# Two kinds of early work moved to VectorE, with a new order of steps, in a fused DeltaNet and feed-forward kernel

## The chip, the cores and the metric

The kernel runs on one core of one Trainium2 chip. The metric is device time in microseconds (us), the median of several executions. Every execution used below for a ratio is in the fast state. A ratio is the mean time of one kernel's fast runs over the mean of the other kernel's fast runs of the same rounds on the same chip, with a 95% interval; it is therefore not quite the ratio of the medians that stand beside it. The kernel before had medians of 611.4 to 614.0 us in the different rounds, so ratios, not medians, are compared across experiments.

## The reference

```python
# q, k, v: (4, 8, 768, 48); beta: (4, 8, 768)
k_n = k / (np.linalg.norm(k, axis=-1, keepdims=True) + 1e-06)
for t in range(S):
    y[:, :, t] = np.einsum('bhd,bhde->bhe', q[:, :, t], state)
    v_old = np.einsum('bhde,bhd->bhe', state, kt)
    state = state + bt[:, :, :, None] * np.einsum('bhd,bhe->bhde', kt, vt - v_old)
# x = y as (3072, 384)
h = (x @ w1) * (x @ w2) @ w3        # w1, w2: 384 x 1024; w3: 1024 x 1024
out = h @ w_out                     # w_out: 1024 x 384
```

The kernel computes the recurrence in 12 chunks of 64 steps. Each chunk needs the inverse of a triangular matrix, built from the scores of K with K (called U). It folds w3 and w_out into one matrix w3·w_out before the feed-forward products start.

## The kernel before

The kernel is a set of named generators. Each `yield` ends a step, and a long string ORDER says in which order the steps are emitted. Every engine then executes its own instructions in that order, as the traces show: in the changed kernel ScalarE ran a copy of w3T at 39.70 us, the three passes of P10 at 40.90 to 42.02 and the second copy of Vb at 42.57, as ORDER has them. The names that matter here: K, Q (transposes), s (scores), V (the inverse of a pair of chunks, "V0" for the first), P0 to P7 (pieces of w_out), P8 to P23 (pieces of w3), t (transpose of a w3 piece), f (fold), p (loads of K and Q in a permuted layout, `kperm` and `qperm`), a (the first feed-forward products, `ab`).

A piece of a weight passes through four engines:

```python
def piece(n, srcs, dst):
    raw = in_turn(ffn, [P, CW, 2], "raw", 5, "raw", U32)
    for rows, src in srcs:
        sync.dma_start(...)                                      # SP's queue
    yield
    ...
    act.activation(out=dst, in_=hi..., func=ACTF.Abs, ...)       # ScalarE, three passes
    act.activation(out=lo, in_=lo, func=ACTF.Copy, ...)
    act.activation(out=hi..., in_=hi..., func=ACTF.Sign)
    yield
    dve.tensor_scalar(out=du, in0=du, scalar1=3, ..., op0=ALU.logical_shift_left)   # VectorE
    yield
    pool.tensor_tensor(out=du, in0=du, in1=lo, op=ALU.add)       # POOL
    pool.tensor_tensor(out=dst, in0=dst, in1=hi..., op=ALU.mult)
    yield
```

The inverse of the first pair runs on VectorE in PSUM, after two ScalarE copies that bring its start matrix Vb there. They are **two separate steps** of the order:

```python
def inverse(j):
    pool.memset(Vb[:], 0.0); ...                                 # step 1
    yield
    sync.dma_start(out=U[:], in_=Uds.pop(j)[:])                  # step 2: Ub
    yield
    if j < 2:
        V = two_banks()...
        for i in range(0, BS, BS // 2):
            act.copy(out=V[:, i : i + BS // 2], in_=Vb[...])     # steps 3 and 4
            yield
    for s in range(BS - 1):                                      # 31 steps of two VectorE operations
        dve.tensor_tensor(out=tv, in0=V[...], in1=U[...], op=ALU.mult)
        dve.tensor_tensor(out=o, in0=o, in1=tv, op=ALU.subtract)
        yield
    ...
```

In ORDER of the kernel before, the two copies are neighbours: `V0 V0`.

## Time and profile before

| | before |
|---|---|
| median (4 runs) | 611.37 us (610.85 to 614.12) |
| span of the profiled run, clock | 608.8 us, 0.969 |
| PE busy, idle | 569.2 us, 39.6 us |
| VectorE, ScalarE, POOL busy | 323.8, 183.4, 145.0 us |
| first inverse step on VectorE | 41.85 us |
| first `ab` product | 130.69 us |

Three readings carry the rest. PE's busy time is the work, as long as it took at the clock that was granted. Span minus PE busy is idle time (the prediction's 39.8 counts to 609.0 us), and all but 4.8 us of it lies in the first 180 us. In a timeline line, the first two numbers are start and duration of a group of equal instructions; the brackets at its end hold the idle time of that engine just before, and what ended it. The prediction below shows the profile's lines themselves; two that it lacks are the first inverse step and the first fold product (VectorE, then PE, of the kernel before):

```profile
41.85 0.19 DVE L434 TENSOR_TENSOR tb<-ps_w,Ub 128x31 f32<-128x31 f32 x1 [1.22 <-DMA Ub<-Ud]
...
45.74 4.77 PE L722 MATMUL ps_f<-w2s,w3T 128*128 128x384 f32 x8 [0.47 <-ACT w3T L716]
```

One warning on the clock columns, here and in the prediction: the trace's records of the granted clock begin only at 22.3 us in the kernel before and at 26.7 us in the changed kernel, and the views print 1.00 where there is no record. TensorE was slow there all the same: in the changed kernel a w3 transpose took 418 ns at 10 us, 417 ns at 39 us, where the record says 0.50, and 273 ns at 28 us, where it says 1.00.

### The profile page before, as it was taken

How to read it: one execution, taken by the hardware profiler on the slowest of the kernel's cores; microseconds unless marked ns; L12 is line 12 of the kernel's file. 1: busy time of each engine (PE TensorE's matmuls, PEld its weight loads, DVE VectorE, ACT ScalarE, POOL GpSimd, SP SyncE). 2: the span in 40 equal slices, each digit the busy share in tenths (PEclk: the TensorE clock that was granted, in tenths of full speed). 3: DMA queues.
4: the chain of work that ended last, by engine and by line, in shares of the span. 5: the costliest groups of instructions: out<-in, count | busy, mean ns of one | idle time of the engine just before them, and what ended most of it. 6: DMA issues, size and time to landing. Idle time of an engine off the chain costs nothing.

```text
span 608.8 us, 17988 instructions
## 1 busy us (share of the span) xinstructions
PE 569.2 (94%) x7804; PEld 333.2 (55%) x7804; DVE 323.8 (53%) x752; ACT 183.4 (30%) x373; POOL 145.0 (24%) x150
## 2 busy tenths in 40 slices
PE   3728998989999999999999999999999999999997
PEld 3724666644566545566555655566545564654454
DVE  2659975578745954766964539675384231101100
ACT  3677656754451012211102321123210113121100
POOL 5778866576340010200031001310000000000000
PEclk9856997999999999999999999999999999999999
DMA  9678678868764342725444354253102110000001
GB/s 200 163 192 230 189 144 172 200 143 156 135 124 86 88 81 27 124 51 111 95 88 64 48 109 99 54 84 60 48 21 86 31 33 1 27 29 13 1 13 39
DMA packets 202223, 55.67 MB, mean 91 GB/s; under 512 B 192352, under 2 KB 195424, under 8 KB 202144
## 3 DMA queue, kind: packets, MB, share of 16 engines
q1 hardware_dynamic: 197952, 53.74, 41.7%
q10 hardware_dynamic: 4192, 0.79, 1.0%
q8 instruction: 61, 1.00, 0.7%
q14 instruction: 18, 0.15, 0.1%
HBM read 42.30 MB, written 11.01 MB: 88 GB/s over the span
## 4 chain that ended last, share of the span: by engine, by line
PE 71%; DMA 8%; SPq 8%; DVE 6%; POOL 2%; issue 2%; ACT 1%; POOLq 0%; DVEq 0%; ACTq 0%
PE ps_f L742 36%; PE ps_f L762 21%; SPq L226 4%; PE ps_w L517 4%; PE ps_w L618 3%; DMA raw<-in_moe_w_dram 2%; PE ps_t L487 2%; SPq L663 2%; PE ps_w L366 2%; PE ps_t L473 1%; PE ps_w L360 1%; DVE ps_w L439 1%; DVE tb L434 1%; DMA Ub<-Ud 1%; DVE w L675 1%
## 5 line engine op out<-in xcount | busy, mean ns | idle before, releaser
L742 PE MATMUL ps_f<-xT,w2s 128*128 128x512 f32 x288 | 132.7, 600 | 0.2 <-POOL w2s L678 0.2
L742 PE MATMUL ps_f<-xT,w1s 128*128 128x512 f32 x288 | 131.1, 598 | 1.6 <-DMA xT<-xT 1.6
L762 PE MATMUL ps_f<-w,ab 128*128 128x384 f32 x384 | 127.3, 488 | 0.0
L762 PEld LDWEIGHTS ps_f<-w,ab 128*128 128x128 f32 x384 | 72.3, 190 | 50.9 <-issue 3.8
L756 DVE TENSOR_TENSOR ab<-a,ps_f 128x512 f32<-128x512 f32 x48 | 32.8, 686 | 126.0 <-PE ps_f L742 123.6
L742 PEld LDWEIGHTS ps_f<-xT,w1s 128*128 128x128 f32 x288 | 53.4, 190 | 62.9 <-issue 56.6
L742 PEld LDWEIGHTS ps_f<-xT,w2s 128*128 128x128 f32 x288 | 52.8, 190 | 59.3 <-issue 55.5
L751 ACT COPY a<-ps_f 128x512 f32<-128x512 f32 x48 | 27.5, 585 | 144.8 <-PE ps_f L742 140.5
L266 POOL TENSOR_TENSOR sq<-ktok 128x384 f32<-128x384 f32 x24 | 20.6, 858 | 156.5 <-DVE ss L268 98.9
L722 PE MATMUL ps_f<-w2s,w3T 128*128 128x384 f32 x128 | 48.9, 536 | 2.1 <-ACT w3T L716 2.1
L503 POOL TENSOR_TENSOR vtok<-vtok,n 128x384 f32<-128x384 f32 x24 | 19.6, 836 | 128.7 <-DMA vtok<-in_v_dram 128.7
L434 DVE TENSOR_TENSOR tb<-Vb,Ub 128x31 f32<-128x31 f32 (+15 forms) x124 | 43.5, 351 | 7.1 <-DMA Ub<-Ud 3.1
L639 ACT COPY xT<-ps_w 48x256 f32<-48x256 f32 x96 | 30.4, 365 | 50.1 <-PE ps_w L618 35.3
L439 DVE TENSOR_TENSOR Vb<-Vb,tb 128x31 f32<-128x31 f32 (+15 forms) x124 | 43.0, 347 | 4.3
L768 ACT COPY osb<-ps_f 128x384 f32<-128x384 f32 x24 | 11.4, 479 | 109.6 <-PE ps_f L762 81.5
L722 PEld LDWEIGHTS ps_f<-w2s,w3T 128*128 128x128 f32 x128 | 25.8, 209 | 19.9 <-issue 3.9
L360 PE MATMUL ps_w<-KQ 48*64 48x128 f32 x384 | 30.9, 306 | 3.9 <-ACT KQ L343 3.4
L360 PEld LDWEIGHTS ps_w<-KQ 48*64 48x64 f32 x384 | 25.8, 152 | 9.7 <-ACT KQ L343 4.0
L366 PE MATMUL ps_w<-KQ 48*64 48x64 f32 x768 | 30.9, 241 | 0.0
L581 DVE TENSOR_TENSOR S<-S,ps_w 48x768 f32<-48x768 f32 x20 | 19.0, 949 | 19.3 <-PE ps_w L517 14.4
L366 PEld LDWEIGHTS ps_w<-KQ 48*64 48x64 f32 x768 | 28.5, 153 | 0.1
L713 PE MATMUL ps_f<-ident,w 128*128 128x128 f32 x64 | 11.4, 320 | 14.4 <-POOL w L678 12.1
(94 smaller groups left out, 642.9 us busy)
## 6 DMA issues: line engine op xcount, KB each, us to landing
raw<-in_moe_w_dram SPq DMA_DIRECT2D x16, 512.0 KB, 4.7
vtok<-in_v_dram SPq DMA_DIRECT2D x24, 192.0 KB, 4.0
raw<-in_moe_w_dram SPq DMA_DIRECT2D x24, 192.0 KB, 3.9
out_dram<-osb SPq DMA_DIRECT2D x24, 192.0 KB, 1.9
ktok<-in_k_dram SPq DMA_DIRECT2D x44, 96.0 KB, 3.2
raw<-in_moe_w_out_dram SPq DMA_DIRECT2D x8, 384.0 KB, 4.9
Ud<-U SPq DMA_DIRECT2D x48, 64.0 KB, 2.0
Ub<-Ud SPq DMA_DIRECT2D x6, 512.0 KB, 3.5
```

Of the source, the lines that this page charges most:

```text
L226: sync.dma_start(out=dst[quarter(2 * e + j), :, :, tb, 0:nd].rearrange("t b a d -> t (b a) d"), in_=src.rearrange("b (a e) t d -> e (b a) ...
L360: pe.matmul(ps[half(z), 0, n : n + 128], lhsT=x[:, 0, :], rhs=x.rearrange("p j t -> p (j t)"), start=True, stop=True,)
L366: pe.matmul(ps[half(z ^ j), 1, n + C * j : n + C * j + C], lhsT=x[:, 0, :], rhs=x[:, j, :], start=True, stop=True,)
L434: dve.tensor_tensor(out=tv, in0=V[:, 0 : s + 1, s : s + 1].to_broadcast([P, s + 1, n]), in1=U[:, s, s + 1 : BS].unsqueeze(1).to_broadcast( ...
L439: dve.tensor_tensor(out=o, in0=o, in1=tv, op=ALU.subtract)
L517: pe.matmul(out(ps, r, h, z), lhsT=lhs(r, h, z), rhs=rhs(r, h, z), start=True, stop=True,)
L639: act.copy(out=xT[f, p:NP:2, b : b + NR, cc, :].rearrange("p a r t -> p r a t"), in_=pyv[f, z, b : b + NR],)
L722: pe.matmul(ps[:, 0:DM], lhsT=w3Ts[jc, kc // 4][:, kc % 4 * P : kc % 4 * P + P], rhs=wo[:, kc], start=(kc == 0), stop=(kc == KF - 1),)
L742: pe.matmul(ps[:], lhsT=w[:, m, js], rhs=x[:, m].rearrange("p b c t -> p (b c t)"), start=(m == 0), stop=(m == KM - 1),)
L751: act.copy(out=a[:], in_=ps[:])
L756: dve.tensor_tensor(out=t[:], in0=a[:], in1=ps[:], op=ALU.mult)
L762: pe.matmul(ps[:, 0:DM], lhsT=abs_[u, jc][:, b * P : (b + 1) * P], rhs=w34[:, jc, :], start=(jc == 0), stop=(jc == KF - 1),)
```

## The change

The change has three parts: VectorE makes the masked scores of chunks 0 and 1 straight from PSUM, in a step (`x0`, `x1`) apart from U and later; VectorE puts the sign bits into the pieces of w_out with one bitwise operation, in place of a ScalarE pass and a POOL product; and ORDER is written anew. The intent is to relieve ScalarE and POOL in the first 60 us, to have U sooner, and so to start inverse and fold sooner.

```diff
-    def scores(m):
+    def scores(m, js=(0, 1)):
...
-            if m < 2:
-                act.copy(out=by_parity(PT), in_=psv[:, :, :, 1, :])
-                yield
-                pool.tensor_tensor(
-                    out=PT, in0=PT, in1=smask[:].unsqueeze(1).to_broadcast([P, H, C]), op=ALU.mult
-                )
-            else:
+            if 1 in js:
+                if r == 0:
+                    PTs[m] = in_turn(work, [P, NR, H, C], "PT", 3, "PT")
                 dve.tensor_tensor(
...
-        act.activation(out=hi.bitcast(FP32), in_=hi.bitcast(FP32), func=ACTF.Sign)
+        if not early:
+            act.activation(out=hi.bitcast(FP32), in_=hi.bitcast(FP32), func=ACTF.Sign)
         yield
         dve.tensor_scalar(out=du, in0=du, scalar1=3, scalar2=None, op0=ALU.logical_shift_left)
+        if early:
+            dve.scalar_tensor_tensor(
+                out=du, in0=hi, scalar=0x80000000, in1=du, op0=ALU.bitwise_and,
+                op1=ALU.bitwise_or,
+            )
         yield
         pool.tensor_tensor(out=du, in0=du, in1=lo, op=ALU.add)
-        pool.tensor_tensor(out=dst, in0=dst, in1=hi.bitcast(FP32), op=ALU.mult)
+        if not early:
+            pool.tensor_tensor(out=dst, in0=dst, in1=hi.bitcast(FP32), op=ALU.mult)
...
+        parts[f"s{m}"] = lambda m=m: scores(m, (0, 1) if m > 1 else (0,))
+        parts[f"x{m}"] = lambda m=m: scores(m, (1,))                      # m = 0, 1
```

And of the order (all of it is new; cut to the stretch that will matter):

```diff
-t2 P13 N0 V0 V0 P4 P4 P4 P1 P1 P3 P3 P13 s1 v0 V0 t5 V0 V0 V0 t2 t5 V0 V0 ...
+N0 P22 u0 u1 P6 P1 P1 P0 V0 P23 P23 Q0 Q0 Q0 Q0 g1 P22 V0 P22 P23 P6 P6 P0 P0 P0 P2 P2 t5 t5
+P22 t14 t14 Q0 P10 P10 V0 V0 P6 V0 V0 q1 V0 V0 ...
```

In the first new line the second `V0` is the first copy of Vb. In the second new line the first `V0` is the second copy. Seventeen steps stand between them.

## The prediction

> **What bounds the kernel now.** The median is 611.84 us; the profiled execution spans 608.8 us. First the page's shares and slices:
>
> ```profile
> PE 569.2 (94%) x7804; PEld 333.2 (55%) x7804; DVE 323.8 (53%) x752; ACT 183.4 (30%) x373; POOL 145.0 (24%) x150
> ...
> PE   3728998989999999999999999999999999999997
> PEclk9856997999999999999999999999999999999999
> ```
>
> TensorE is full from the third quarter of the first 180 us on. What it loses, it loses at the start, by idleness and by a lower granted clock. The table by stage (columns: stretch, length, busy time of PE, PEld, DVE, ACT, POOL with counts, granted clock, DMA share, GB/s) sizes both:
>
> ```profile
> 0.00:15.00 15.00, 5.53 (x142) 4.57 (x146) 3.11 (x6) 5.34 (x9) 7.89 (x18) 1.00 1.10 199
> 15.00:30.00 15.00, 11.48 (x307) 10.59 (x303) 10.27 (x27) 10.00 (x19) 11.08 (x12) 0.86 0.65 169
> 30.00:45.00 15.00, 4.68 (x53) 3.59 (x45) 7.98 (x20) 11.35 (x23) 12.00 (x11) 0.50 0.77 181
> 45.00:60.00 15.00, 11.77 (x24) 6.14 (x23) 14.24 (x33) 11.81 (x22) 13.08 (x13) 0.62 0.87 233
> 60.00:75.00 15.00, 14.71 (x57) 9.16 (x56) 14.24 (x34) 9.14 (x18) 12.33 (x12) 1.00 0.71 201
> ...
> 90.00:105.00 15.00, 12.09 (x307) 9.61 (x306) 8.22 (x15) 9.78 (x21) 11.52 (x10) 0.77 0.85 178
> ...
> 180.00:240.00 60.00, 59.88 (x762) 34.25 (x753) 37.23 (x86) 10.68 (x23) 4.40 (x5) 1.00 0.37 73
> ```
>
> Idle is length less PE busy; busy time times (1 - clock) estimates what slow clock costs. Idle: 9.5, 3.5, 10.3, 3.2, 0.3, then 2.9 in 90 to 105 and 5.1 in the rest up to 180; about 1.4 from 180 to 540, 3.6 in the tail. Slow clock: 1.6, 2.3, 4.5 in the three stretches from 15 to 60, 2.8 in 90 to 105. The loss is 39.8 + 11.2 = 51 us, of which **15 to 60 us holds 25.5**. PE's own waits name the cause:
>
> ```profile
> PE ps_f L713 <- POOL w L678: 12.1, 3, 5.3
> PE ps_f L333 <- DMA ktok<-in_k_dram: 7.3, 3, 4.7
> PE ps_w L360 <- ACT KQ L343: 3.4, 2, 2.9
> ```
>
> L713 transposes a piece of w3, which POOL (L677, L678) must have decoded. Each piece passes DMA, ScalarE, VectorE and POOL, and the fold (L722, 8 times 8 matmuls; 8 matmuls take 5.7 us at full clock) needs all eight w_out pieces. So the first 60 us are a chain of preparation, the rest is TensorE work.
>
> [...] idle gaps of 4.98 and 5.34 us before L713, clock 0.50. [...] the trace has 687 (L374) and 550 (L560). [...] the same 128x512 shift L675 means 867 ns for w3, beside a busy POOL, and 467 for w1. [...]
>
> **The change, part by part.** Durations by shape, 0 to 200 us:
>
> ```profile
> L678 POOL TENSOR_TENSOR w2s<-w2s,raw 128x384 f32<-128x384 f32 x8 | 8.3, 1041 | 0.6
> L392 DVE TENSOR_TENSOR PT<-ps_w,smask 128x512 f32<-128x512 f32 x8 | 5.4, 680 | 0.0
> L388 POOL TENSOR_TENSOR PT<-PT,smask 128x512 f32<-128x512 f32 x4 | 5.1, 1280 | 0.6 <-ACT PT L386 0.6
> L673 ACT ACTIVATE raw<-raw 128x384 f32<-128x384 f32 x8 | 4.4, 548 | 0.0
> L560 DVE TENSOR_TENSOR X<-ps_w,wt 128x384 f32<-128x384 f32 x8 | 4.1, 550 | 2.3 <-PE ps_w L517 2.3
> L386 ACT COPY PT<-ps_w 128x512 f32<-128x512 f32 x4 | 2.3, 583 | 5.1 <-DVE U L374 5.1
> ```
>
> - Signs of w_out: POOL loses 8 x 1.041 = 8.3 us, ScalarE 8 x 0.548 = 4.4, VectorE gains 8 operations, estimated at L560's 0.55 = 4.4.
> - Masked scores of chunks 0 and 1: ScalarE loses 4 x 0.583 = 2.3 us, POOL 4 x 1.28 = 5.1; VectorE gains 4 x 0.68 = 2.7. TensorE gets 4 x 8 more, narrower matmuls over the same columns: about 0.
> - Sum: **POOL -13.4 us, ScalarE -6.7, VectorE +7.1**. POOL is busy 85 of the first 120 us, so most of its saving becomes waiting unless the order uses it.
> - The order of steps. Before, K0, Q0, K1 and Q1 come first and scores wait for them; U of chunk 1 ends at 32.1. After, TensorE does one w3 transpose, then K0, K1 and both U-scores; q0 is loaded later, w_out comes as P7, P1, P6, P0, P2, P3, P5, P4.
>
> I walked the new order by hand with the durations above. **Norms and U.** The first w3 piece lands near 6 us, POOL has it at 10.3, K0 and K1 end at 15.4, the last sum of squares at 17.2. Across, seed (0.2 to 1.7) and the fourteen short operations (3.3) put the scale at about 22.5 (before 24.1). U ends at about 26.4 against 32.1, gain 5.7. **Inverse of the first pair**: Ub lands at 36.7 against 41.8; the 62 steps (22 us without interruption) plus some 7 us of decoding between them, as before, end at 65.5 against 70.9. **Last w_out piece**: its DMA (41st in SP's order, behind eight kperm loads at 0.5) is issued at about 46, lands at 51, passes VectorE between inverse steps by 53.5 and POOL by 54.5. Before, it was issued at 44.1 and POOL was done at 55.1. So the fold's full run starts about where it did; first halves of two folds start at about 49[...].
>
> By 65 us I find TensorE ahead by only about 1 us; by 80 even (x0 and x1 are then done, one transpose and half of s2 are not). **Here I choose**: the gain is later. From 80.7 us to the first ab matmul (130.7) TensorE lost 8.8 us: w3T and KQ waits at 92 to 98 and their slow clock, xT at 128.9 (1.6). In the new order V0, TT, Vd and POOL's w3 pieces come 4 to 5 us ahead of need, and 12 fold matmuls (8.5 us) and one product stand between y1 and the first ab, so the xT transfer hides. I take 6 to 7 of these 8.8 as saved and 1 given back, where w2's pieces, which overwrite w_out, wait for the last fold and only three jc of w1 work (8 us) cover them. Sum: 0.5 + 6.5 - 1 = 6. 611.84 - 6 = **605.5 us**.
>
> **Rivals.**
> 1. *The wait only changes its name* (no gain, 609 to 614). For: the last w_out piece is POOL-done within 1 us of before, and VectorE, at 14.2 of 15 us in 45 to 75, gets more work, decoding between inverse steps. Against: V0 starts earlier[...].
> 2. *The early stage really shortens* (594 to 600). For: POOL -13.4 us just where PE waits 12.1 us for POOL[...]. Against: SP issues in order, raw has five buffers, and wo loads behind Ud, Ub and kperm come as late as before.
> 3. *VectorE becomes the bound* (612 to 618): +7.1 us ahead of V1. Against: VectorE idles 7 of 15 us in 30 to 45, and 6.8 in 90 to 105.
>
> **Range and chances.** Main case 602 to 609, weight 0.55; rival 1 about 0.25; rival 2 about 0.15; rival 3 0.05. That gives 599.5 to 612 for 8 in 10. Faster by 2% means under 599.6, a quarter of the 51 us gone: 0.16. Slower by 2% (over 624) would need a new stall: 0.02.
>
> **What would show it.** Right: PE busy after 180 us as before; POOL busy near 132, VectorE near 331; the first Ub-dependent VectorE step at 36 to 38; the first fold matmul at 48 to 51; the first ab matmul at 123 to 127, with clock 1.00 from 55 on and no xT wait. Wrong: L724 first runs before 45 (rival 2); the first ab stays at 130 (rival 1); VectorE decoding ends the PE waits (rival 3). My weakest step is the hand walk of landings, each good to 2 or 3 us.

## The result, and the profile after

| | before | after |
|---|---|---|
| median (4 runs each) | 611.37 us | 621.95 us (620.25 to 622.29) |
| ratio of fast runs | | **1.0158** (1.0122 to 1.0195) |
| span of the profiled run, clock | 608.8, 0.969 | 620.5, 0.967 |
| PE busy, idle | 569.2, 39.6 | 568.5, 52.0 |
| VectorE, ScalarE, POOL busy | 323.8, 183.4, 145.0 | 329.7, 177.5, 132.2 |

The change is 1.6% slower. PE's work is the same within 1 us, its idle time is 12.5 us larger. The page of the changed kernel, shares and the PE slices:

```profile
PE 568.5 (92%) x7868; PEld 331.9 (53%) x7868; DVE 329.7 (53%) x764; ACT 177.5 (29%) x361; POOL 132.2 (21%) x138
...
PE   3535967999899999999999999999999999999997
...
PEclk9956999899799999999999999999999999999999
```

The fourth slice, at 46.5 to 62 us, is the new hole: 5 tenths, where the kernel before had 8. The same table by stage as in the prediction, for the changed kernel (stretch, length, busy time of PE, PEld, DVE, ACT, POOL, granted clock, DMA share, GB/s):

```profile
30.00:45.00 15.00, 5.07 (x104) 4.14 (x104) 4.79 (x12) 9.00 (x18) 7.50 (x7) 0.50 1.04 259
45.00:60.00 15.00, 7.02 (x18) 4.43 (x19) 14.06 (x38) 7.84 (x15) 6.59 (x7) 0.59 0.56 156
...
105.00:120.00 15.00, 12.27 (x191) 8.17 (x183) 3.48 (x6) 8.71 (x17) 8.69 (x8) 0.89 0.72 156
...
180.00:240.00 60.00, 59.77 (x857) 34.59 (x859) 36.07 (x85) 12.14 (x29) 3.20 (x5) 1.00 0.41 81
```

VectorE is the surprise. It was busy for 7.98 us of 30 to 45 before, and is busy for only 4.79 now, though it has more to do: something holds it. PE had 11.77 in 45 to 60 and has 7.02. From 180 us on PE is as full as before (idle for 4.8 us there in both kernels). PE's own waits in the changed kernel (in total, times, longest):

```profile
PE ps_f L715 <- POOL w L680: 28.9, 4, 9.8
PE ps_w L512 <- issue: 4.5, 1, 4.5
PE ps_w L367 <- issue: 2.7, 1, 2.7
...
PE ps_f L744 <- DMA xT<-xT: 1.3, 1, 1.3
```

The wait for POOL, which the change was to shorten, has grown from 12.1 to 28.9 us (one of its four parts, 9.3 us, is the kernel's start, where the kernel before waited for ktok instead). Two waits named "issue" are new: there TensorE waited for nothing that the profile shows. By shape, the removed and added operations:

```profile
L678 POOL TENSOR_TENSOR w2s<-w2s,raw 128x384 uint32<-128x384 uint32 x8 | 8.3, 1041 | 24.0 <-DVE w2s L673 22.4 <-issue 1.6
...
L673 DVE SCALAR_TENSOR_TENSOR w2s<-raw,w2s 128x384 uint32<-128x384 uint32 x8 | 5.4, 679 | 0.3
```

The new L673 took 0.56 us in most cases (estimate 0.55); the mean of 0.679 has one of 1.52 us in it, at 26.93 us, while POOL ran L680 and L266. POOL's column at the right says where its saving went: 22.4 us of waiting for L673. The timeline of the changed kernel shows why VectorE stood still (ScalarE, then VectorE, then PE):

```profile
39.70 0.58 ACT L718 COPY w3T<-ps_f 128x512 f32<-128x512 f32 x1 [2.59 <-PE ps_f L715]
...
42.02 0.65 ACT L669 ACTIVATE raw<-raw 128x512 f32<-128x512 f32 x1
42.57 0.59 ACT L423 COPY ps_w<-Vb 128x512 f32<-128x512 f32 x1
...
43.19 0.19 DVE L429 TENSOR_TENSOR tb<-ps_w,Ub 128x31 f32<-128x31 f32 x1 [8.45 <-ACT ps_w L423]
...
38.55 1.11 PE L715 MATMUL ps_f<-ident,w 128*128 128x128 f32 x4 [9.80 <-POOL w L680]
...
52.98 1.11 PE L715 MATMUL ps_f<-ident,w 128*128 128x128 f32 x4 [8.10 <-POOL w L680]
53.89 2.76 PE L724 MATMUL ps_f<-w2s,w3T 128*128 128x384 f32 x4
```

Read it from the third line up. The first inverse step came at 43.19 after 8.45 us of idleness, and what released it was not Ub, which had landed at 34.6, but L423, the second copy of Vb. That copy of 0.59 us needs nothing that was late. It stands on ScalarE behind w3T's copy L718, which waited for the transpose at 38.55, which had waited 9.80 us for POOL to decode P22. So the inverse started 1.3 us later than in the kernel before, though its data had come 7 us sooner; it ended at 70.9 us, as before. What came late was the work between its steps: VectorE's decoding steps stand there, so they were late, and with them POOL's next w3 piece, the transpose at 52.98 and the fold at 53.89 (45.74 before).

The two waits named "issue" lie in the middle of runs of equal matmuls of the changed kernel:

```profile
91.31 0.97 PE L512 MATMUL ps_w<-vtok,TT 64*64 64x48 f32 x30 [4.51 <-issue]
...
108.34 0.21 PE L367 MATMUL ps_w<-KQ 48*64 48x64 f32 x1 [2.73 <-issue]
```

In each of them the trace's DMA records have one packet of 16 KB of the kind "instruction" (at 88.86 for 1.10 us, at 105.85 for 1.15 us). The DMA part of the page says how many there are in the changed kernel (packets, MB, share):

```profile
q8 instruction: 62, 1.02, 0.7%
```

The numbers fit TensorE's stream: the changed kernel has 7868 matmuls, and as many weight loads, and q8 carried 62 packets with 1.02 MB; the kernel before has 7804 and 61 packets. That is one packet for 127 or 128 pairs of load and matmul. I took each packet for a refill of TensorE's instructions, and call the pairs that it serves a block; the size of a block is my estimate from these counts, and the page doesn't name the engine that a packet is for. So two suspects were in hand: the late copy, and waits for TensorE's own instructions.

### The profile page after: what moved, and what is told of

It reads as the page before. It is cut to its first block, busy times and chain, and to the rows that moved or that the text cites. A ratio compares the mean times of both kernels' runs of the same rounds, so it can differ in the third digit from the quotient of the medians.

```text
span 620.5 us, 18105 instructions
## 1 busy us (share of the span) xinstructions
PE 568.5 (92%) x7868; PEld 331.9 (53%) x7868; DVE 329.7 (53%) x764; ACT 177.5 (29%) x361; POOL 132.2 (21%) x138
## 3 DMA queue, kind: packets, MB, share of 16 engines
q8 instruction: 62, 1.02, 0.7%
## 4 chain that ended last, share of the span: by engine, by line
PE 76%; DVE 6%; SPq 3%; issue 3%; DMA 3%; ACT 2%; DVEq 0%; ACTq 0%
PE ps_f L744 37%; PE ps_f L764 20%; PE ps_w L512 5%; PE ps_w L613 3%; PE ps_f L724 3%; SPq L226 3%; PE ps_t L482 2%; DVE tb L429 2%; PE ps_t L468 2%; DVE ps_w L434 2%; PE ps_w L361 1%; PE ps_w L367 1%; PE ps_f L715 1%; DMA Vd<-Vb 1%; DVE KQ L320 1%
## 5 line engine op out<-in xcount | busy, mean ns | idle before, releaser
L744 PE MATMUL ps_f<-xT,w1s 128*128 128x512 f32 x288 | 133.8, 609 | 1.3 <-DMA xT<-xT 1.3
L744 PE MATMUL ps_f<-xT,w2s 128*128 128x512 f32 x288 | 131.9, 599 | 0.0
L744 PEld LDWEIGHTS ps_f<-xT,w1s 128*128 128x128 f32 x288 | 53.9, 193 | 61.6 <-issue 57.9
L753 ACT COPY a<-ps_f 128x512 f32<-128x512 f32 x48 | 27.3, 586 | 143.1 <-PE ps_f L744 132.4
L266 POOL TENSOR_TENSOR sq<-ktok 128x384 f32<-128x384 f32 x24 | 20.5, 855 | 156.6 <-DVE ss L268 106.3
L434 DVE TENSOR_TENSOR Vb<-Vb,tb 128x31 f32<-128x31 f32 (+15 forms) x124 | 44.7, 360 | 4.3
L498 POOL TENSOR_TENSOR vtok<-vtok,n 128x384 f32<-128x384 f32 x24 | 20.2, 858 | 123.7 <-DMA vtok<-in_v_dram 53.9
L715 PE MATMUL ps_f<-ident,w 128*128 128x128 f32 x64 | 11.7, 317 | 29.0 <-POOL w L680 28.9
L367 PE MATMUL ps_w<-KQ 48*64 48x64 f32 x896 | 29.5, 237 | 3.0 <-issue 2.7
L429 DVE TENSOR_TENSOR tb<-ps_w,Ub 128x31 f32<-128x31 f32 (+15 forms) x62 | 21.0, 339 | 15.3 <-ACT ps_w L423 8.4
L367 PEld LDWEIGHTS ps_w<-KQ 48*64 48x64 f32 x896 | 26.4, 150 | 0.8 <-DVE U L376 0.4
L678 POOL TENSOR_TENSOR w<-w,raw 128x512 uint32<-128x512 uint32 x16 | 20.8, 1298 | 23.4 <-PE ps_f L715 8.2
```

Source lines behind the costliest of these rows:

```text
L266: pool.tensor_tensor(out=sq[:], in0=kt[:, r], in1=kt[:, r], op=ALU.mult)
L367: pe.matmul(ps[half(z ^ (j & h)), h % 2, n + C * j : n + C * j + C], lhsT=x[:, 0, :], rhs=x[:, j, :], start=True, stop=True,)
L429: dve.tensor_tensor(out=tv, in0=V[:, 0 : s + 1, s : s + 1].to_broadcast([P, s + 1, n]), in1=U[:, s, s + 1 : BS].unsqueeze(1).to_broadcast( ...
L744: pe.matmul(ps[:], lhsT=w[:, m, js], rhs=x[:, m].rearrange("p b c t -> p (b c t)"), start=(m == 0), stop=(m == KM - 1),)
L753: act.copy(out=a[:], in_=ps[:])
```

## The experiments

All kernels below gave correct results. In this summary "issue" is the sum of PE's waits with that name, in us, in the one execution that was profiled, "V0" the first inverse step on VectorE, and "ab" the first `ab` product; the medians are in us, with the kernel before of the same rounds beside them (they include the few slow runs, such as two each in e10 and e16; the ratios don't).

| run | median / before | ratio (95%) | issue | V0 | ab |
|---|---|---|---|---|---|
| e1_signs | 615.21 / 613.74 | 1.0008 (0.9985–1.0032) | 1.4 | | 132.8 |
| e2_masks | 611.28 / 613.74 | 0.9967 (0.9944–0.9989) | 1.9 | | 129.7 |
| e3_signs_masks | 613.47 / 613.74 | 0.9992 (0.9963–1.0021) | 1.7 | | 130.0 |
| e4_copy_early | 615.96 / 613.74 | 1.0026 (1.0006–1.0046) | 5.1 | 35.80 | 131.1 |
| e5_mirror | 617.90 / 613.63 | 1.0071 (1.0037–1.0104) | 0.9 | 46.75 | 137.6 |
| e6_phase48 | 618.72 / 613.63 | 1.0078 (1.0040–1.0116) | 12.1 | | 134.4 |
| e7_phase88 | 623.86 / 613.63 | 1.0157 (1.0121–1.0192) | 7.9 | | 131.6 |
| e8_calm | 619.16 / 613.63 | 1.0089 (1.0054–1.0123) | 2.0 | | 135.8 |
| e9_calm_act | 613.80 / 613.79 | 0.9997 (0.9974–1.0020) | 3.1 | 33.83 | 130.9 |
| e10_calm_pool | 614.88 / 613.79 | 0.9997 (0.9973–1.0022) | 3.7 | | 131.9 |
| e11_before_phase48 | 632.99 / 613.79 | 1.0298 (1.0236–1.0359) | 13.3 | | 131.2 |
| e12_calm_alone | 619.97 / 613.79 | 1.0087 (1.0060–1.0114) | 2.9 | 43.45 | 137.7 |
| e13_before_phase24 | 617.98 / 611.93 | 1.0109 (1.0065–1.0154) | 3.4 | | 132.4 |
| e14_before_phase72 | 614.71 / 611.93 | 1.0046 (1.0027–1.0066) | 1.2 | | 134.8 |
| e15_calm_phase24 | 619.86 / 611.93 | 1.0147 (1.0096–1.0197) | 5.5 | | 131.9 |
| e16_calm_phase72 | 612.12 / 611.93 | 0.9996 (0.9981–1.0012) | 0.5 | 33.60 | 128.7 |
| e19_after_phase72 | 620.42 / 614.01 | 1.0094 (1.0064–1.0125) | 5.8 | 42.01 | 139.0 |
| e20_copy_phase72 | 614.68 / 614.01 | 1.0001 (0.9974–1.0028) | 5.4 | 36.65 | 132.2 |

For comparison: before 0.6, 41.85, 130.7; the changed kernel 1.0158, 7.2, 43.19, 138.2.

### The parts alone: e1_signs, e2_masks, e3_signs_masks

The two swaps of engine are put into the kernel before, alone and together, with its old order. (In e2 the masked scores are made in the old place, not apart from U.)

```diff
 # e1_signs: the diff of piece() above, on the kernel before
 # e2_masks: in scores() of the kernel before, for all chunks
-            if m < 2:
-                act.copy(...); yield; pool.tensor_tensor(...)
-            else:
-                dve.tensor_tensor(out=by_parity(PT), in0=psv[:, :, :, 1, :], in1=smask..., op=ALU.mult)
+            dve.tensor_tensor(out=by_parity(PT), in0=psv[:, :, :, 1, :], in1=smask..., op=ALU.mult)
+            if m < 2:
+                yield
 # e3_signs_masks: both
```

> The kernel before with the w_out signs by VectorE alone, its order of steps kept. Theory A (the new order of steps costs the time, above all the wait of the first inverse's VectorE steps for the second copy into PSUM): 604 to 612 us, no loss. Theory B (VectorE's added work, 8 operations of 0.56 us, is on the path): 614 to 620 us.

> The kernel before with the masked scores of chunks 0 and 1 made by VectorE in place of ScalarE and POOL, still right after U, order kept. Theory A: 608 to 613 us, since 4 operations of 0.68 us replace 4 copies and 4 masks beside the path. Theory B (VectorE's work is on the path): 614 us or more.

> Both changes of engine with the order of before. Theory A: 603 to 612 us, so that the new order alone holds the loss of 10 us. Theory B: about 620 us, the time of the changed kernel, with the old order.

Ratios 1.0008, 0.9967 and 0.9992. In microseconds e1 (615.21) fell into the range of theory B, and e3 (613.47) above that of theory A, but the kernel before stood at 613.74 in the same rounds, higher than the expectations assumed; the ratios decide. The swaps cost nothing and together gain nothing that can be told from zero, although in e3 POOL lost 12.0 us of work (145.0 to 133.0). e2_masks, the masks alone in the old order, is the only version here whose interval lies below 1 against the kernel before; it is 0.3% faster than that, and so also the fastest beside the changed kernel. **The whole loss of 1.6% is in the new order** (with the split of the scores into two steps that belongs to it, and that no run took alone).

### One step moved: e4_copy_early, and its mirror e5_mirror

```diff
 # e4_copy_early: ORDER of the changed kernel
-... P22 V0 P22 P23 P6 P6 P0 P0 P0 P2 P2 t5 t5 P22 t14 t14 Q0 P10 P10 V0 V0 P6 ...
+... P22 V0 V0 P22 P23 P6 P6 P0 P0 P0 P2 P2 t5 t5 P22 t14 t14 Q0 P10 P10 V0 P6 ...
 # e5_mirror: ORDER of the kernel before; the second copy behind two w3T copies
-... N0 V0 V0 P4 P4 P4 P1 P1 P3 P3 P13 s1 v0 V0 t5 V0 V0 V0 t2 t5 V0 V0 ...
+... N0 V0 P4 P4 P4 P1 P1 P3 P3 P13 s1 v0 t5 t2 t5 V0 V0 V0 V0 V0 V0 V0 ...
```

> The changed kernel with one step moved: the second ScalarE copy of the first inverse into PSUM follows the first at once, and no longer stands behind the w3 transpose that waits for POOL. Theory A: the inverse's first VectorE step moves from 43.2 to about 35 us, the third w3 transpose in the gap before the fold from 53.0 to about 46, and the time falls to 611 to 616 us. Rival C (the loss lies later, in stalls of TensorE near 87 and 106 us that the profile puts down to issue): the inverse starts earlier, but the time stays at 619 to 622 us.

> The kernel before, with one thing of the new order put into it: the second ScalarE copy of Vb, which the first pair's inverse needs, moved behind two w3T copies in ScalarE's order (and the two pairs of inverse steps between with it). Theory A (a copy that stands late in ScalarE's in-order queue holds the inverse and all behind it): the first inverse step on VectorE starts near 46.5 to 47 us instead of 41.85, the inverse ends 4 to 5 us later than 70.9, the first ab matmul moves from 130.7 to 134 or later, and the time rises by 3 to 6 us (ratio 1.005 to 1.010). Theory B (the copy was harmless, and the other moves of the new order cost the time): time within 1.5 us of before.

Moving the one step took the ratio from 1.0158 to 1.0026. In e4 the inverse waits for its data, and the third w3 transpose follows the second with little idleness (VectorE, then PE, of e4_copy_early):

```profile
35.80 0.19 DVE L429 TENSOR_TENSOR tb<-ps_w,Ub 128x31 f32<-128x31 f32 x1 [1.01 <-DMA Ub<-Ud]
...
45.62 1.11 PE L715 MATMUL ps_f<-ident,w 128*128 128x128 f32 x4 [0.69 <-POOL w L680]
...
84.61 0.61 PE L512 MATMUL ps_w<-vtok,TT 64*64 64x48 f32 x26 [2.85 <-issue]
```

The transpose came at 45.62 instead of 52.98, and the first `ab` product at 131.1 instead of 138.2. The mirror put the same fault into the good kernel, and the same wait appeared (ScalarE, then VectorE, of e5_mirror):

```profile
46.12 0.59 ACT L428 COPY ps_w<-Vb 128x512 f32<-128x512 f32 x1
...
46.75 0.19 DVE L434 TENSOR_TENSOR tb<-ps_w,Ub 128x31 f32<-128x31 f32 x1 [5.43 <-ACT ps_w L428]
```

V0 started at 46.75 (expected 46.5 to 47), the ab product came at 137.6 (expected 134 or later), and the time rose by 4.3 us in the medians (expected 3 to 6), with issue waits of only 0.9 us. The late copy is shown from both sides to cost time: in the changed kernel 0.0132 of 613 us, 8 us; with two loads moved (e12 against e9, below) 0.9%. What e4 did not bring is the predicted gain, and its last line above shows a stop that has nothing to do with the copy.

### Where TensorE stops without a named reason: e6_phase48 and e7_phase88

If the stops are refills, they must hang on the count of TensorE's instructions, not on the place in the program. Tiny transposes in TensorE's first idle 9 us shift the count.

```diff
 # on e4_copy_early, in transpose_w3(), for the first piece only (48, or 88)
+        if 2 * jc + hf == 4:
+            for x in range(48):
+                pe.transpose(ps[0:64, x % 4, 0:64], ident[0:64, 0:64], ident[0:64, 0:64])
```

> The changed kernel with the second copy early, plus 48 tiny transposes (64x64 of the identity, into a bank that the real transposes then overwrite) on TensorE at the start, where it idles for 9 us. They shift by 48 matmuls where the instruction refills fall in TensorE's stream. Theory C (the stops of 2.85 us inside L512 and of 2.20 us inside L367 are waits for TensorE's own instructions): each stop moves to another place of the program, about 48 matmuls earlier (counted with the extra ones it stays near 854 and 1235), or vanishes because the refill now meets less DMA traffic. Theory D (they are waits for data or registers that the profile doesn't name): the stops stay before the same matmuls of the program, that is at counts 902 and 1283. Time between -5 and +2 us of the kernel without the transposes (615.96).

> As e6_phase48 with 88 transposes. Theory C: the stops, if there are any, stand at the same count of matmuls with the extra ones in it (near 854 and 1235, plus whole periods of about 125), so at another place of the program than in the kernel without them; a refill packet lies in each. Theory D: counts 942 and 1323.

Timeline of PE in e6_phase48:

```profile
84.51 0.37 PE L482 MATMUL ps_t<-TT,T 32*32 32x32 f32 x5 [4.76 <-issue]
...
103.22 0.33 PE L361 MATMUL ps_w<-KQ 48*64 48x128 f32 x2 [3.22 <-issue]
```

The stops left L512 and L367 and went to other lines, L482 and L361. Counted in matmul records, they are before number 855 and 1236; in the changed kernel and in e4 they are before 854 and 1235. Had they kept their place in the program, they would be at 902 and 1283. In e7 the longest, 2.05 us, lies before 1109. The grid holds in every kernel that I looked at:

```text
number of the matmul record before which TensorE stopped (waits named issue of over 1.1 us; e15's at 855 was 0.4)
changed kernel, e4          854, 1235
e6 (+48), e15 (+48)         855, 1236, 5432
e7 (+88)                    1109, 2380, 6195, 6703
e9                          1108
e19 (+144), e20 (+144)      982; e20 also 1744
e11 (kernel before, +96)    854, 2378, 2885, 3522, 4158, 6066
steps: 982-854 = 128; 1109-982 = 127; 1235-1108 = 127; 2885-2378 = 507, about 4 x 127; 4158-2885 = 1273, about 10 x 127
```

That is the block of some 127 matmuls that the packet counts gave, and shows that the stops are tied to the instruction stream, and with a refill packet in each of the long ones, or begun up to 1.5 us before it, that they are waits for instructions. e6's time rose by 2.8 us above e4's, where at most 2 were expected; its stops were longer (12.1 us in all instead of 5.1), but its profiled run was the slowest of its eight. e7 was not foreseen in its time: no stop of it was over 2.1 us, but it was 1.3% slower than e4. Its 88 transposes lasted longer than the idle time that they were to fill, so that Q, K and all behind them came some 1.7 us late, and its granted clock was 0.56 in 90 to 105 us (0.73 in e4). I did not take this further.

The trace also says how the wait comes about. I read from it when TensorE crossed each block boundary, and when the next refill packet started:

```text
                          crossed    refill started   after   block lasted
changed kernel, block 6     82.86        88.86         6.00      3.72   -> stop 4.51
changed kernel, block 9    101.28       105.85         4.57      4.11   -> stop 2.73
changed kernel, block 19   186.92       188.27         1.35      4.98   no stop
changed kernel, block 25   245.70       246.21         0.51      7.52   no stop
e16, block 7                75.51        77.46         1.95      3.82   no stop
```

In eight kernels with nearly 500 refills, no packet started more than 1.2 blocks before TensorE reached its block, and some started only when TensorE stood at it. From the twentieth refill on, where DMA traffic is light (DMA share 0.34 from 192.5 to 540 us in the changed kernel), the median start was 0.6 to 1.0 us after the crossing; in the two stops it was 6.0 and 4.6, and the DMA share from crossing to start was 1.02 and 0.92. A block of small matmuls lasts some 4 us (block 6: 127 records in 3.72 us), so there TensorE can run dry. So it was at all 28 stops of over 1.1 us in the changed kernel, e4 and e6 to e20: among the 127 matmuls before each there was no fold or feed-forward product, and they lasted 1.9 to 4.4 us (once 6.4). But a short block is not enough: the kernel before has four of 2.1 us, from 193 us on, with no stop behind them.

### Taking traffic away: e8_calm, e9_calm_act, e10_calm_pool, e12_calm_alone

```diff
 # e8_calm: on e4, the loads of P20 and P21 (512 KB each) behind the sixteen kperm and qperm loads
-... P20 t0 t8 c0 s2 s2 t0 P17 P17 P17 P18 f0 P21 t8 c0 c0 P21 P21 p3 p3 y0 ... s2 P20 P25 ...
+... t0 t8 c0 s2 s2 t0 P17 P17 P17 P18 f0 t8 c0 c0 p3 p3 P21 P20 y0 ... s2 P20 P21 P21 P25 ...
 # e9_calm_act: the ScalarE and VectorE steps of P20 and P21 later still, behind V1 s2 s2 P19
+... p3 p3 P20 P21 y0 ... V1 s2 s2 P19 P20 P21 P20 P21 P20 P24 P21 s3 ...
 # e10_calm_pool: e9, and POOL's step of P22 before that of P0
 # e12_calm_alone: e9's moves of P20 and P21 on the changed kernel, second copy still late
```

> The changed kernel with the second copy early, and two 512-KB loads of w3 (P20 and P21) moved behind the sixteen kperm and qperm loads of the same stretch, so that less is queued on the DMA rings at 75 to 82 us. Theory C with DMA traffic as the cause of the late refill: the refill that lies in the first stop starts earlier against the matmuls, the stop of 2.85 us shrinks below 1, and the time falls by 1 to 3 us. If the refill's lateness does not come from those loads: the stop stays at matmul 854 or within 10 of it, at 2 to 4 us, and the time is within 1 us of 615.96.

> The changed kernel with the second copy early and the loads of P20 and P21 behind kperm and qperm (as e8_calm), but with the ScalarE passes of P20 and P21 also moved behind the T copies of chunk 1, so that they don't hold these up. In e8_calm both stops at refills (2.85 and 2.20 us) were gone, but TensorE waited 5.79 us at L361 for a T copy that stood behind the late pieces on ScalarE. If that wait is all that took the gain away, this kernel shows neither it nor the stops, and the time falls 3 to 7 us below e8_calm's, to 611 to 615 us (ratio 0.998 to 1.003). If the ratio stays near 1.009, the stops were not worth their length.

> e9_calm_act with POOL decoding the w3 piece P22 before the w_out piece P0, for which POOL stood idle 1.80 us while P22 was ready for it. The wait of TensorE before transpose t14 falls from 9.35 to about 6.5 us. If that gap sets the end, the time falls by up to 3 us; if the fold's start is set by the landing of w_out's pieces (47 to 48 us), the gap only moves on and the time stays within 1 us of e9_calm_act.

> The changed kernel with the moves of P20 and P21 alone (the second copy of Vb as late as in the change). If the two causes add, the stops at refills (4.51 and 2.73 us in the changed kernel) go, the first inverse step stays at 43.2, the first ab matmul comes at 131 to 133 instead of 138.2, and the time is 615 to 618 us (ratio 1.004 to 1.009), about as good as the early copy alone. If the refills are no cause of their own, it stays at 621 to 622.

In e8 both stops were gone, as the traffic theory says (one of 1.99 us came at the grid's 1108), but the time rose to 1.0089: I had made the first fault again. PE waited 5.79 us at L361 for a copy of T on ScalarE, and that copy stood at 101.09 behind the three passes each of P20 and P21, which began only when P20's load had landed at 97.6. e9 put these passes behind the T copies. The 5.79 us and both stops were gone, the stop at 1108 took 2.79 us, and the ratio was 0.9997. The expectation of 611 to 615 us was met.

e12 leaves the copy late and moves the loads only: both stops went (one of 2.7 us came at the 1108 of e9), V0 stayed at 43.45, and the ratio was 1.0087 (expected 1.004 to 1.009). The median of 619.97 us lay above the 615 to 618 expected, and the first `ab` product came at 137.7, not at 131 to 133: it hangs on the late copy. So each of the two moves brings the time of the changed kernel down: 1.0158 with neither, 1.0087 with the loads moved, 1.0026 with the copy early, 0.9997 with both. They don't add exactly: moving the loads is worth 0.7% with the late copy, and 0.3% with the copy early, where the two intervals overlap, so that this part is not clear of noise. That the shorter stops are what pays is argued, not shown: see e19 below.

In e10 TensorE's wait for P22 fell from 9.35 to 6.84 us, yet the ratio stayed at 0.9997. The gap before Q0's transposes (L333) grew from 1.27 to 2.34, one of 2.57 came before the next w3 transpose, and PE's waits for POOL at L715 were 20.4 us in all, against 20.5 in e9. The fold did not start sooner (46.5 us in e9, 47.8 in e10, of which 1.0 was there at 17 us already). The POOL saving of 12.8 us could not shorten the early stage here.

### Is the kernel before itself lucky: e11_before_phase48, e13_before_phase24, e14_before_phase72, and the mended order: e15_calm_phase24, e16_calm_phase72

A call of a plain fp32 matmul gives two records here (24 calls are 48 records in e13, which took 1.53 us, and 72 calls 144 in e16), so 24, 48 and 72 calls shift the count by 48, 96 and 144; the last is a whole block and some 17.

```diff
 # e11, e13, e14: by_tensor() of the kernel before, K of chunk 0 only (48, 24 or 72 calls)
+        if m == 0 and i == 0:
+            for r in range(24):
+                pe.matmul(ps[...], lhsT=ident[...], rhs=ident[...], start=True, stop=True)   # overwritten later
 # e15, e16: the same in transpose_w3() of e9, before the first w3 piece (24 or 72 calls)
```

> The kernel before with 48 tiny matmuls at the start, in TensorE's first 5 us of idleness (their results are overwritten). Theory C says that the kernel before is free of stops at refills between 80 and 120 us only by where its refills fall: with the shift, one or two stops of 1 to 4 us with no releaser named turn up in 75 to 125 us or at 24 us, each with a refill packet in it, and the time rises by 1 to 5 us. If the kernel before is robust, no new stop appears and the time is within 1.5 us of before.

> The kernel before with 24 tiny matmuls at the start[...]; refills fall 24 matmuls earlier in the program. If the kernel before sits at a lucky place, as its 3% loss with 48 suggests: 1 to 3% slower (618 to 632), with waits named issue of 2 us or more in sum and a refill packet in the longest. If 48 was itself an unlucky place: within 0.5% of before.

> As e13 with 72. Lucky place: 0.5 to 3% slower. Unlucky 48: within 0.5%.

> The changed kernel with both causes mended (e9_calm_act), with 24 tiny matmuls before the first w3 transpose, in TensorE's first 9 us of idleness. If the place of the refills eats the missing gain: at one of the two shifts (24, 72) the stop of 2.79 us at matmul 1108 goes and no other comes, and the time is 606 to 610 (ratio 0.988 to 0.995). If the gain was never there: both shifts give 0.998 or more.

> As e15 with 72: 606 to 610 if the place of the refills eats the gain and this is a good place; 614 to 625 if it is a bad one; stops, where there are any, stand at the same counts as before modulo the period of some 125 matmuls, with a refill packet in them.

The 48 calls made the kernel before 3.0% slower, more than the change did, and its first `ab` product still came at 131.2: nearly all of the 18 us between the profiled spans was lost later, with waits named issue of 13.3 us in all against 0.6. A rise of 1 to 5 us was expected. 24 calls cost 1.1%, 72 calls 0.5%, which is on the line between what a lucky and an unlucky place were said to give. They are not free in themselves: with 72, the first inverse step was pushed from 41.9 to 44.3, which may be all of that 0.5%. Even so the kernel before stands at a good place: none of three shifts did as well. The new order with both causes mended spreads the same way: 1.0147 with 24 calls and stops of 5.5 us, 0.9996 with 72 calls and 0.5 us. The expectation for e16 of 606 to 610 us was missed: the profiled run had a span of 606.2 us, but the median of 20 runs was 612.12. Both e15 and e16 lie above 0.998, which e15's text had set as the mark of "the gain was never there". **Freed of both causes and of all stops, the new order ties with the old.**

### The shift without any moved load: e19_after_phase72 and e20_copy_phase72

```diff
 # e19: e16's 72 calls on the changed kernel as it is; e20: the same on e4_copy_early
```

> The changed kernel, not one step moved, with the 72 tiny matmul calls (144 records) in TensorE's first 9 us of idleness. If the stops of 4.51 and 2.73 us come from where refills fall: both go, waits named issue fall from 7.2 us to under 2, the first inverse step stays at about 43 us, and the time falls from 622 to 615 to 618 (ratio 1.004 to 1.010). If they come from the order itself: issue waits of 5 us or more stay, and the ratio stays at 1.014 or more.

> The changed kernel with the second copy of Vb early and the same 72 calls, no load moved. If the late copy and the place of the refills are the two causes: issue waits under 2 us, ratio 0.992 to 1.001, as good as the kernel with the loads moved too (0.9996). If the moved loads matter for themselves: 1.002 or more.

I expected the issue waits to fall below 2 us in both, and was wrong: 5.8 and 5.4. The stops at 854 and 1235 had gone, but at the next boundary of the grid, 982, a new one stood at nearly the same place of the program. e16, with the same shift, has no stop there. The only thing between e20 and e16 is the place of the loads and decode steps of P20 and P21. SP's queue in e20_copy_phase72, then the stop:

```profile
76.57 1.39 SPq L658 DMA_DIRECT2D raw<-in_moe_w_dram  x3
78.05 8.89 SPq L226 DMA_DIRECT2D kperm<-in_k_dram  x8
```

```profile
85.28 1.00 PE L512 MATMUL ps_w<-vtok,TT 64*64 64x48 f32 x28 [2.90 <-issue]
```

and SP's queue in e16_calm_phase72:

```profile
72.90 0.43 SPq L658 DMA_DIRECT2D raw<-in_moe_w_dram  x1
73.43 5.96 SPq L226 DMA_DIRECT2D kperm<-in_k_dram  x8
```

With two loads fewer ahead of them, the eight kperm loads were issued in 5.96 instead of 8.89 us, and the refill for the block at 982 started when TensorE had 37 matmuls left (at number 945), not when it had run out. So the place of a refill alone does not make a stop: here a short block and heavy traffic met it (DMA share 0.98 in 80 to 85 us of e20, 0.78 in 75 to 80 us of e16, where that refill started). In time, e19 is at 1.0094 (expected 1.004 to 1.010) and e20 at 1.0001 (expected 0.992 to 1.001); e20 equals e16 within the intervals, so that its stops (2.9 and 1.95 us, against 0.5 us in all) are not seen in the time. Nor does e19's gain of 0.6% over the changed kernel come with shorter stops in sum (5.8 us against 7.2). A second thing came with the 72 calls: e19's first record of full clock is at 5.7 us, the changed kernel's at 26.7, and the first 66 K transposes took 1.20 us instead of 2.15. Shift and clock changed together in e11, e14, e16, e19 and e20, and what the shift alone is worth there is not shown.

## Why the prediction was wrong

The prediction was 605.5 us with a range of 599.5 to 612; the result is 621.95. Step by step:

- **The costs of the operations** were right: VectorE 329.7 (about 331 said), POOL 132.2 (132), ScalarE down by 5.9 (6.7), the new operation 0.56 us (0.55). TensorE's 64 more matmul records did not lengthen its busy time (568.5 us, 569.2 before). PE busy after 180 us is as before. e1 to e3 show that these costs lie beside other work, as the prediction said of "most of" POOL's saving.
- **Norms and U** were right: U ended at 25.6 us (about 26.4 said).
- **"Inverse of the first pair: Ub lands at 36.7 … end at 65.5"** failed. Ub landed even sooner, at 34.6, but the inverse began at 43.2 and ended at about 70.9, where it had ended in the kernel before. I took the landing of Ub for the only thing that the first step waits for. The order had split the two copies of Vb by seventeen steps, and I did not look at where the second one stands on ScalarE's queue. e4 and e5 show that this step is worth 8 of the 16 us that the prediction missed by.
- **"The first fold matmul at 48 to 51"** failed for the same reason (53.9): the VectorE steps that decode w3's piece P10 stood behind the inverse. With the copy early it was 48.1.
- **"I take 6 to 7 of these 8.8 as saved"** failed independently. This is the term that stays missing when both causes are mended. In e9, from 80 to 131 us, PE was idle for 5.3 us and lost 6.9 us to the clock (45.74 us busy at 0.85), 12.1 in all; the kernel before, in the same stretch, lost 5.4 and 3.2, 8.6 in all. Nothing of the 8.8 was saved; the wait for xT was still 1.5 us in e9, and the first `ab` product came at 130.9, in e16 at 128.7, not at 123 to 127. e16 lost 10.3 in 80 to 129. The stops at refills, a term that the sum did not have at all, took 7.2 us in the changed kernel and 3.1 in e9. The clock fell with one of them: in e9 it was 0.50 from 94.8 us, just after the stop of 2.79 us, to 105.1, which makes about 5 of the 6.9 us. Why it stayed low for 10 us, and was low from 77.8 to 84.6, stays open.
- **The reading of the clock** was off, though it did not enter the 605.5: there is no record before 22.3 us, and 12.8 us of PE work there ran slow (matmuls of L360 took 417 ns in the median, as they did at 26 to 35 us, where the record says 0.50, and 269 ns at 22.4 to 25.7, where it says 1.00), and the 0.50 that it sets beside gaps of 4.98 and 5.34 us had begun at 25.8 us, before both. By the prediction's own rule that is some 6 us more loss, about 57 instead of 51.
- **Rival 1** ("the wait only changes its name") named the right mechanism, but not that it could cost: its range ended at 614. Rival 2 did not come (first fold at 53.9, not before 45), and e10 shows that POOL's earlier work did not start the fold sooner; rival 3 is refuted by e3 for the old order. "Slower by 2% would need a new stall" had chance 0.02; new stalls came, and the time rose by 1.6%.

The change is slower by less than 2%, and "neither 2% faster nor slower" had 0.82; the number was out of its range by 10 us.

What stays open: when TensorE asks for a refill is not in the trace, only when the packet starts. That traffic delays it rests on the stop near 75 to 90 us, which five kernels with the two loads moved did not have (e8, e9, e10, e12, e16; a sixth, e15, had 0.4 us there, and 2.5 later), against the changed kernel, e4, e6, e19 and e20, which had it at 2.9 to 4.8 us; but e7, with no load moved, had 0.3 us there and 2.05 us at 91. e11 has stops of up to 2.1 us after 180 us, where traffic is lighter (DMA share 0.27 to 0.42 in 180 to 540 us, against 0.69 and more in 60 to 180), so traffic is not the only thing that makes them. How much of the time the stops cost is open too: issue waits of 5.5 us stand beside 1.0147 in e15, and 5.4 beside 1.0001 in e20. And why the best shift still doesn't bring the new order ahead of the old is settled only as a sum of the stretch above, not by a run.

## What to carry to other kernels

Before believing that work starts when its data lands, list everything that the first instruction reads, and find the last of it in the order of *its* engine: a copy of 0.6 us behind a late wait on ScalarE's queue cost 0.9 to 1.3% of the whole kernel. When TensorE stops inside a run of equal small matmuls and the profile names no releaser, count the matmuls: here the stops lay on a grid of about 127 records and had an instruction packet in or just before them, 48 more records at the start (e6) put them on other lines of the program, and with two loads moved (e8) the one of 2.85 us was gone. Two orders of one kernel that differ by 1% should be compared at more than one shift, since tiny calls at the start were worth up to 3% here (e11; with 72 of them the first record of full clock came earlier as well, at 5.7 us in e19).

## What the traces show of refills and the clock

- Refills. Single crossings of a block boundary cost up to 4.8 us (e6) where blocks of small matmuls lasted some 3 to 4 us, and waits named issue came to 13.3 us in one kernel (e11). In nearly 500 refills none started more than 1.2 blocks ahead.
- Refills and traffic. The packet started 0.6 to 1.0 us (median) after the crossing in light traffic, and 4.6 and 6.0 us after it in the two stops.
- The clock. In the kernel before and the changed kernel every record of the granted clock but the last lasts a multiple of 3.41 us (3.41, 6.83, 23.89 and 37.55 us among them). In the changed kernel the clock was 0.50 from 91.5 us, after a stop of 4.51 us, and from 108.6 us, after a gap of 2.73 us. In e16 it was 0.50 from 90.7 us, for 6.83 us, though no gap of the 20 us before was over 0.45 us. So what makes it fall is not shown here.
- Records of the clock. They can begin late (22.3 us in the kernel before, 52.4 in e4, 45.8 in e6), and the views then show full clock. In e4 four w3 transposes took 1.11 us at 28.1, 38.6 and 45.6 us, and 0.60 us at 61.3, where the record says 1.00: TensorE ran slow before.
